# Attention with two-key pooled queries and a gated MLP on one core: products for the maxima inside the groups of scores, two chunks ahead, and values two chunks behind

## The chip, the cores and the metric

One Trainium2 chip, one of its cores. The metric is the time of one execution on the device in microseconds (us), as a median over runs; beside it stands one execution taken with the hardware profiler.

## What is computed

```python
def _attn_ref(q, k, v):                 # q, k, v: 8 x 8 x 1152 x 64, f32
    B, H, S, D = q.shape
    q_pool = q.reshape(B, H, S // 2, 2, D).mean(axis=3)      # 576 queries
    scores = np.matmul(q_pool, k.transpose(0, 1, 3, 2)) / np.sqrt(D)
    scores = scores - np.max(scores, axis=-1, keepdims=True)
    attn = np.exp(scores)
    attn = attn / (np.sum(attn, axis=-1, keepdims=True) + 1e-09)
    return np.matmul(attn, v)

def _moe_ref(x, w_in, w_spatial, b_spatial, w_out):   # x: 8 x 576 x 512
    h = np.maximum(x @ w_in, 0.0)                      # 512 -> 1024
    u, v = h[..., :512], h[..., 512:]
    v_n = (v - mean(v)) / sqrt(var(v) + 1e-06)
    v_s = np.einsum('ts,bsd->btd', w_spatial, v_n) + b_spatial[None, :, None]
    return (u * v_s) @ w_out
```

x is the attention's output with its heads side by side. Results are held to f32 accuracy, so most products are made of three f16 products of high and low halves.

## The kernel before, in words

**Blocks and chunks.** The attention runs over 32 blocks (8 batches times 4 pairs of heads, `NP`). Within a block the 1152 keys are 9 chunks of 128 (`NC`). One chunk is: `scores(i, c)` (line 894), 12 products on TensorE that use 64 rows of the array for each of the two heads, into the tile `pss` (3 PSUM banks, one buffer); one Exp on ScalarE over 1152 columns into `pt` (line 905, 4 buffers); `split(i, c)` (line 913), which takes the low half of `pt`, on GpSimd for eight chunks and on VectorE for one; `values(i, c)` (line 811), 27 products of 128 rows into the tile `o` (2 banks, one buffer). Values lag the scores by one chunk (`LAG`, line 750, used in `attention`). In the first 8 blocks (`EARLY`) three of the nine chunks skip the split, and their values are f32 products.

**The maxima of the next block.** The Exp needs a shift per query, made from the largest score. `maxima(i)` (line 695) computes the scores once more in one f16 product, in 9 pieces of 512 columns for both heads: a pair of 64-row products (two pairs where a piece crosses a tile of queries; line 705) writes both banks of the tile `pm`, and VectorE reduces both heads in one instruction of up to 2 x 512 elements (line 710). Two tail products follow (128 rows, line 717), with their reductions (718). `shift(i)` (line 721) takes the maximum of the pieces (726), writes factors into `wide` (729, 737), turns them with six small products (743, 745), and copies them to `sh` (746, 747). The first chunk's scores of the block read `sh`. The tile `pm` (two banks, one buffer, made by `pair_of_banks`) also serves small jobs: sums for scales, the variance of the MLP, a transposition.

**Where they are put.** The loop at the end makes the generator `ahead_of(i + 1)`: nine pieces, tails, shift. Each of block i's nine chunks steps it once after its scores, and `drain(nxt)` at the end of the block runs what is left: tails and shift. So block i + 1 begins behind them in the program.

**The other work.** `prep(i + 2)` and `steps_of_k(i + 1)` make the f16 halves of queries and keys (line 666 takes a difference of keys on VectorE, 456 and 459 are squares and halves on ScalarE), `values_ahead` those of v (621, 622 and, on GpSimd, 624), all stepped at fixed rates per chunk; the weights are loaded and turned from f64 in the first blocks (474 to 486). Every 8 blocks a `gated_unit`, the MLP of two batches, becomes ready: it makes products into `pw` (one bank, lines 968, 1032, 1083, 1092, 1130), stepped about 20 times per block. The last unit has nothing beside it and runs at the end in all free banks.

**What sets the order.** `Order.pin` takes the whole program and lays it out by list scheduling: it has a cost per instruction, due times, and per engine a list of the ready ones; the earliest start wins, then the lowest number in the program. The order found is then fixed on each engine's queue, which runs in order. Tiles of one name must begin in the order of the program, and a tile waits for all users of the one that had its buffer. A `bundle` is a row of TensorE products placed without a break: the 12 of a chunk's scores, or those of one piece of the maxima. Going from 128-row products to a bundle costs the planner 100 ns for scores and 1500 ns for maxima (`APART`), so it waits that long for something of the same kind.

Of the kernel before, what the change touches and what calls it, by code (L numbers as in the profile page):

```python
# [31 lines left out]
class Order:  # L32
# [8 lines left out]
    APART = {"scores": 100, "maxima": 1500}  # L41
    SIZE = {F16: 2, BF16: 2, F32: 4, I32: 4, U32: 4, I64: 8}

    def __init__(self):
        self.slot = {}
        self.count = {}
        self.lined = []
        self.seen = 0
        self.bundles = []
        self.plan = []  # L50
# [20 lines left out]
    @contextmanager  # L71
    def bundle(self, tc, part):
# [3 lines left out]
        self.bundles.append((part, names))  # L76
# [130 lines left out]
    def pin(self, tc):  # L207
# [18 lines left out]
        members, wait = {}, [0.0] * len(prog)  # L226
        for part, ns in self.bundles:
            ns = [place[x] for x in ns]
            members[ns[0]] = [(n, bool(prog[n].ins) and self.access(prog[n].ins[0])[3] >= 64) for n in ns]
            wait[ns[0]] = self.APART[part]  # L230
            for n in ns:
                lead[n] = ns[0]
# [19 lines left out]
        def placed(n, t, end):  # L252
            e = lane[n]
            if e in last:
                tc.add_manual_dep(prog[n], last[e], dep, reason="order")
            last[e] = prog[n].name
            self.plan.append((prog[n].name, t, end))
            for m, through in after[n]:
                k = lead[m]
                left[k] -= 1  # L260
                if not through:
                    x = t
                elif lane[m] != e:
                    x = end + self.DELAY.get((e, lane[m]), 52)
                else:
                    x = t if e == "PE" else end + 34
                there[k] = max(there[k], x)
                due[k] = max(due[k], x + (self.SLACK.get((e, lane[m]), 0) if through else 0))
                if not left[k]:
                    ready[lane[k]].append(k)  # L270

        while any(ready.values()):
            best = None
            for e, ns in ready.items():
                if ns:

                    at = {n: max(due[n], wire - 1000) if n in load else due[n] for n in ns}
                    if e == "DVE":
                        for n in ns:
                            if shared[n] and max(free[e], at[n]) + self.GRAB >= held[0]:  # L280
                                at[n] = max(at[n], held[1] - 175)
                    elif e == "PE":
                        for n in ns:
                            if (n in members) != halves:
# [10 lines left out]
            if e == "PE":  # L295
                if (n in members) != halves:
                    t = max(free[e] + self.SWITCH, t)
                    halves = not halves
                row, at = [t, t], t
# [27 lines left out]
def attn_sgu_kernel(ctx: ExitStack, tc: tile.TileContext, qT, kT, v, w_in, w_spT, b_sp, w_out, out):  # L327
    nc = tc.nc
    P = 128
# [31 lines left out]
    ps_m = order.pool(ctx.enter_context(tc.tile_pool(name="ps_m", bufs=1, space=PSUM)), 1, True)  # L361
# [62 lines left out]
    def pair_of_banks():  # L424
        return ps_m.tile([P, 2, 512], F32, name="pm")

    def short():
        return pair_of_banks()[:, 0] if units else ps_w.tile([P, 512], F32, name="pw")
# [265 lines left out]

    def maxima(i, banks=None):
# [3 lines left out]
        for n, cols in enumerate(PIECES):  # L699
            pm = banks(n) if banks else pair_of_banks()  # L700
            with order.bundle(tc, "maxima"):
                for t, _, y, z, a in cols:
                    for h in range(2):
                        q = t * P if h == 0 or t < 3 else ROLL + TAIL
                        nc.tensor.matmul(  # L705
                            pm[:, h, a : a + z - y], lhsT=qhi[HEADS[h], q : q + P], rhs=khi[HEADS[h], y:z],
                            start=True, stop=True,
                        )
            for t, k, y, z, a in cols:
                nc.vector.reduce_max(out=mt[:, t : t + 5 : 4, k], in_=pm[:, :, a : a + z - y], axis=AX.X)  # L710
            yield
        for n in range(2):
            pm = banks(n) if banks else pair_of_banks()
            w = 512 if n == 0 else P
            for k in range(2 - n):
                y = (2 * n + k) * 512
                nc.tensor.matmul(pm[:, k, :w], lhsT=qdd, rhs=khi[:, y : y + w], start=True, stop=True)  # L717
            nc.vector.reduce_max(out=mt[:, 8, 2 * n : 2 + n], in_=pm[:, 0 : 2 - n, :w], axis=AX.X)  # L718
        yield

    def shift(i):
        st = state[i]
        mt, w, out = st["mt"], wide[i % 2], sh[i % 2]
        pm = pair_of_banks()
        m = pm[:, 1, 384 : 384 + NT]
# [15 lines left out]
        yield  # L741
        for t in range(3):
            nc.tensor.matmul(pm[:, 0, t * P : (t + 1) * P], lhsT=w[:, t], rhs=ident_h, start=True, stop=True)
        for t, e in ((3, eye[:, HALF : 2 * P]), (4, eye[:, 0 : P + HALF]), (5, rest_eye)):
            nc.tensor.matmul(pm[:, 1, 0 : S - CUT], lhsT=w[:, t], rhs=e, start=t == 3, stop=t == 5)
        nc.vector.tensor_copy(out=out[:, CUT:S], in_=pm[:, 1, 0 : S - CUT])
        nc.vector.tensor_copy(out=out[:, 0:CUT], in_=pm[:, 0, 0:CUT])
        yield

    LAG = 1  # L750
# [122 lines left out]
    def scores(i, c):  # L873
# [17 lines left out]
        with order.bundle(tc, "scores"):  # L891
            for _, h, n, dst, w, m, bank in sorted(todo, key=lambda x: x[:3]):
# [22 lines left out]
    def attention(i):  # L915
        for c in range(NC):
            scores(i, c)
# [8 lines left out]
    def gated_unit(un):  # L926
# [58 lines left out]
        pt = pair_of_banks()[:, 0]  # L985
# [208 lines left out]
    def at_start(n):  # L1194
        return pair_of_banks() if n % 2 == 0 else ps_o.tile([P, 2, 512], F32, name="o")
# [8 lines left out]
    first = maxima(0, at_start)  # L1204
# [6 lines left out]
    drain(first)  # L1211
    drain(shift(0))
# [6 lines left out]
    def ahead_of(i):  # L1219
        yield from maxima(i)  # L1220
        yield
        yield from shift(i)

# [5 lines left out]
    nxt = ahead_of(1)  # L1229
    for i in range(NP):  # L1230
# [7 lines left out]
        for at in attention(i):  # L1238
            if at == "scores":
                nxt = step(nxt)  # L1240
# [6 lines left out]
        drain(nxt)  # L1247
        for r in run[:2]:
            drain(r.gen)
        nxt = ahead_of(i + 2) if i + 2 < NP else None  # L1250
# [55 lines left out]
```

## Time and profile before

| what | us |
|---|---|
| median of 2 runs (1427.98 to 1436.63) | 1432.31 |
| the profiled execution's own time | 1430.54 |
| its span, first to last instruction | 1428.8 |
| TensorE, products busy | 1192.4 (83%) |
| VectorE busy | 909.2 (64%) |
| ScalarE busy | 859.1 (60%) |
| GpSimd busy | 718.7 (50%) |
| first Exp starts at | 35.0 |
| last Exp starts at | 1307.8 |

PE is TensorE, PEld its weight loads, DVE VectorE, ACT ScalarE, POOL GpSimd. A busy TensorE in the page counts a product until its result has landed, so products that overlap look long; what a row of products costs is read from the chain of waits, where each stands with the time it added. A releaser is the instruction whose end let a waiting one go.

### The profile page before, as it was taken

The page shows a single profiled execution, that of the slowest core. Times are in us where ns is not written, and L with a number is a line of the kernel's source. Part 1 is how long each engine was busy: PE and PEld are TensorE (multiplying, and loading weights), DVE is VectorE, ACT ScalarE, POOL GpSimd, SP SyncE. Part 2 cuts the span into 40 slices and gives each one's busy share as a digit, 9 for nine tenths or more (in the row PEclk, how much of TensorE's full clock was granted, in tenths as well). Part 3 has the DMA queues.
Part 4 walks back from the last instruction along what each step waited for, and adds up shares of the span by engine and source line. Part 5 has one row for each costly group of instructions (what it writes and reads, how often), then busy time and mean ns, then how long its engine had stood idle before and what let it go on. Part 6 is the DMA issues. An engine that isn't in the chain of part 4 may idle for free.

```text
span 1428.8 us, 33823 instructions
## 1 busy us (share of the span) xinstructions
PE 1192.4 (83%) x14680; PEld 792.6 (55%) x14680; DVE 909.2 (64%) x1640; ACT 859.1 (60%) x1235; POOL 718.7 (50%) x386
## 2 busy tenths in 40 slices
PE   2787777778989897798998886788998888789988
PEld 1575666666546655555555554555655455556443
DVE  7778667865777666865658665575556856561543
ACT  6755566676756666658666665567666465544333
POOL 1444334454646656656666555756766365645000
PEclk9878889989999998799999997899999898899999
DMA  4530421231211222134221122124111020001001
GB/s 158 209 110 34 144 68 68 68 100 44 75 59 40 87 74 77 33 95 131 75 59 45 49 75 75 59 79 151 53 61 59 25 75 9 10 24 53 8 1 67
DMA packets 64118, 99.64 MB, mean 70 GB/s; under 512 B 34016, under 2 KB 34016, under 8 KB 63456
## 3 DMA queue, kind: packets, MB, share of 16 engines
q1 hardware_dynamic: 63968, 97.47, 21.2%
q8 instruction: 115, 1.88, 0.5%
q14 instruction: 35, 0.29, 0.1%
HBM read 81.20 MB, written 9.44 MB: 63 GB/s over the span
## 4 chain that ended last, share of the span: by engine, by line
PE 57%; DVE 20%; ACT 15%; issue 4%; DMA 2%; POOL 2%; ACTq 0%; DVEq 0%; POOLq 0%
PE pss L894 16%; PE o L811 13%; ACT pt L905 8%; DVE mt L710 4%; PE pw L968 4%; PE pw L1130 4%; PE pw L1083 4%; PE pw L1032 4%; PE pm L705 3%; DVE mt L718 2%; DVE kd L666 2%; POOL pt L913 1%; DVE vv L462 1%; PE pm L717 1%; PE pss L968 1%
## 5 line engine op out<-in xcount | busy, mean ns | idle before, releaser
L913 POOL TENSOR_TENSOR pt<-pt 128x1152 f16<-128x1152 f32 x240 | 518.7, 2163 | 550.3 <-ACT pt L905 549.9
L710 DVE TENSOR_REDUCE mt<-pm 128x2 f32<-128x1024 f32 (+1 forms) x380 | 354.2, 952 | 319.5 <-PE pm L705 318.7
L905 ACT ACTIVATE pt<-pss,esc 128x1152 f32<-128x1152 f32 x288 | 350.6, 1218 | 276.9 <-PE pss L894 267.5
L811 PE MATMUL o<-vp,pt 128*128 128x65 f16 (+3 forms) x7128 | 315.9, 199 | 12.9 <-ACT pt L905 10.3
L811 PEld LDWEIGHTS <-pt 128*128 128x128 bf16 (+1 forms) x7128 | 267.3, 99 | 100.0 <-issue 56.7
L894 PE MATMUL pss<-qh,dh 64*128 64x192 f16 (+1 forms) x1152 | 245.8, 307 | 42.4 <-ACT pt L905 40.5
L894 PE MATMUL pss<-qh,dl 64*128 64x192 f16 (+1 forms) x1152 | 244.5, 304 | 0.0
L894 PEld LDWEIGHTS <-dh 64*128 64x128 f16 x2304 | 180.2, 100 | 112.0 <-issue 86.5
L894 PE MATMUL pss<-ql,dh 64*128 64x192 f16 (+1 forms) x1152 | 240.5, 303 | 0.0
L705 PE MATMUL pm<-kh,qh 64*128 64x512 f16 (+1 forms) x760 | 120.7, 348 | 14.2 <-DVE mt L710 10.7
L894 PEld LDWEIGHTS <-dl 64*128 64x128 f16 x1152 | 92.2, 100 | 3.1 <-issue 0.8
L1032 PE MATMUL pw<-xg,wi_h 128*128 128x512 f16 (+1 forms) x304 | 75.8, 332 | 10.9 <-ACT u L1042 10.9
L1130 PE MATMUL pw<-wo_h,vv 128*128 128x512 f16 x216 | 73.3, 391 | 11.9 <-DVE vv L462 6.5
L705 PEld LDWEIGHTS <-qh 64*128 64x128 f16 x768 | 54.7, 99 | 43.9 <-issue 27.3
L968 PE MATMUL pw<-wi_h,xg 128*128 128x512 f16 x224 | 75.2, 379 | 3.2 <-ACT vv L976 2.4
L624 POOL TENSOR_TENSOR vp<-vt,vp 128x576 f16<-128x576 f32 x48 | 68.3, 1432 | 8.4 <-ACT vp L622 8.2
L1083 PE MATMUL pw<-ws_h,vv 128*128 128x512 f16 x192 | 65.5, 393 | 6.1 <-ACT u L1042 3.2
L1083 PEld LDWEIGHTS <-vv 128*128 128x128 f16 x384 | 35.6, 100 | 52.0 <-issue 21.1
L968 PEld LDWEIGHTS <-xg 128*128 128x128 f16 x432 | 38.3, 97 | 43.4 <-issue 8.1
L811 PE MATMUL o<-row,pt 128*128 128x65 f32 (+1 forms) x432 | 58.8, 290 | 3.7 <-ACT pt L905 3.6
L718 DVE TENSOR_REDUCE mt<-pm 128x2 f32<-128x1024 f32 (+1 forms) x63 | 47.8, 759 | 18.9 <-PE pm L717 18.5
L811 PEld LDWEIGHTS o<-row,pt 128*128 128x128 f32 x432 | 54.4, 203 | 7.2 <-ACT pt L905 4.7
(227 smaller groups left out, 1970.1 us busy)
## 6 DMA issues: line engine op xcount, KB each, us to landing
vt<-in_v_dram SPq DMA_DIRECT2D x56, 576.0 KB, 4.2
qt<-in_qT_dram SPq DMA_DIRECT2D x32, 576.0 KB, 4.7
kt<-in_kT_dram SPq DMA_DIRECT2D x32, 576.0 KB, 4.0
out_dram<-row SPq DMA_DIRECT2D x24, 256.0 KB, 2.2
vv<-in_w_in_dram SPq DMA_DIRECT2D x4, 1024.0 KB, 6.5
xg<-in_v_dram SPq DMA_DIRECT2D x4, 576.0 KB, 6.4
vv<-in_w_out_dram SPq DMA_DIRECT2D x2, 1024.0 KB, 6.1
out_dram<-vv SPq DMA_DIRECT2D x8, 256.0 KB, 2.0
```

Of the source, the lines that this page charges most:

```text
L624: nc.gpsimd.tensor_sub(vp[:, h, :, 0:D], vt[:, h], hd)
L705: nc.tensor.matmul(pm[:, h, a : a + z - y], lhsT=qhi[HEADS[h], q : q + P], rhs=khi[HEADS[h], y:z], start=True, stop=True,)
L710: nc.vector.reduce_max(out=mt[:, t : t + 5 : 4, k], in_=pm[:, :, a : a + z - y], axis=AX.X)
L718: nc.vector.reduce_max(out=mt[:, 8, 2 * n : 2 + n], in_=pm[:, 0 : 2 - n, :w], axis=AX.X)
L811: nc.tensor.matmul(dst, lhsT=weights[:, cols], rhs=rhs, start=first and n in (0, 3), stop=last, skip_group_check=True)
L894: x = nc.tensor.matmul(dst, lhsT=w, rhs=m, start=first, stop=n == len(terms) - 1, skip_group_check=True)
L905: nc.scalar.activation(pt.rearrange("p (b q) -> p b q", b=3), ps[:, :, 0:CUT], AF.Exp, bias=0.0, scale=st["esc"])
L913: eng.tensor_sub(pt.bitcast(F16)[:, 0::2], pt, pt.bitcast(BF16)[:, 1::2])
L968: nc.tensor.matmul(ph, lhsT=xa[:, cc, c0 : c0 + P], rhs=wa[:, cc, DH:DF], start=n == 0, stop=n == 3 * NCC - 1,)
L1032: nc.tensor.matmul(pu[:, : z - a], lhsT=wa[:, cc, fc * P : (fc + 1) * P], rhs=xa[:, cc, a:z], start=n == 0, stop=n == 3 * NCC - 1,)
L1083: nc.tensor.matmul(pv, lhsT=l, rhs=r[:, 0:MAIN], start=n == 0, stop=n == len(ts) - 1)
L1130: nc.tensor.matmul(py, lhsT=ga[:, fc, c0 : c0 + P], rhs=wa[:, fc, :], start=m == 0, stop=m == end - 1)
```

## The change

- **Pieces in the groups.** `scores(i, c, piece)` steps the generator of pieces inside its bundle, so that a piece's products are the last members of the group of scores, and steps it again behind the Exp, which emits the piece's reductions. There is always one piece to a chunk.
- **Two chunks ahead.** Two pieces of block 1 are made alone before the loop. After that chunk c of block i carries piece c + 2 of block i + 1, and its chunks 7 and 8 carry pieces 0 and 1 of block i + 2. `prep(i + 2)` is drained at chunk 7.
- **Two tiles of one bank.** The pool of `pm` has two buffers of one bank each instead of one of two banks. Each head of a piece has a tile of its own and is reduced by itself, so a piece takes two reductions (four where it crosses a tile of queries) in place of one (two). The tails are three products with a reduction each.
- **Tails and shift inside the block.** A tail goes behind the scores of chunks 0, 2 and 4, the first half of the shift behind chunk 6, its second half (products and copies) behind chunk 7. Nothing of them is left to the end of a block.
- **Values lag two chunks**; `pt` keeps its 4 buffers.
- **The planner.** Both kinds of switch cost 100 ns; a bundle may start before a late member is due, by the member's place in it; an Exp that comes due within 500 ns goes ahead of another ScalarE instruction that would run into it. `PACE`, `APART`, `URGENT` and `TIGHT` have values with which they change nothing.

```diff
-    APART = {"scores": 100, "maxima": 1500}
+    TIGHT = 0
+    AHEAD = 500
...
+                x -= lag[m]
                 there[k] = max(there[k], x)
...
+                    if e == "Activation":
+                        for m in ns:
+                            if m in prime and t < at[m] <= t + self.AHEAD and t + cost[n][0] > at[m]:
+                                n, t = m, at[m]
...
-    ps_m = order.pool(ctx.enter_context(tc.tile_pool(name="ps_m", bufs=1, space=PSUM)), 1, True)
+    ps_m = order.pool(ctx.enter_context(tc.tile_pool(name="ps_m", bufs=2, space=PSUM)), 2, True)
...
+    def one_bank():
+        return ps_m.tile([P, 512], F32, name="pm")
...
+    def maxima_alone(i, banks, n):
+        gen = maxima(i, banks)
+        for _ in range(n):
+            with order.bundle(tc, order.SWITCH):
+                next(gen)
+            next(gen)
+            yield gen
+
     def maxima(i, banks=None):
...
-            pm = banks(n) if banks else pair_of_banks()
-            with order.bundle(tc, "maxima"):
-                for t, _, y, z, a in cols:
-                    for h in range(2):
-                        q = t * P if h == 0 or t < 3 else ROLL + TAIL
-                        nc.tensor.matmul(
-                            pm[:, h, a : a + z - y], lhsT=qhi[HEADS[h], q : q + P], rhs=khi[HEADS[h], y:z],
-                            start=True, stop=True,
-                        )
-            for t, k, y, z, a in cols:
-                nc.vector.reduce_max(out=mt[:, t : t + 5 : 4, k], in_=pm[:, :, a : a + z - y], axis=AX.X)
-            yield
...
+            pms = banks(n) if banks else (one_bank(), one_bank())
+            for t, _, y, z, a in cols:
+                for h in range(2):
+                    q = t * P if h == 0 or t < 3 else ROLL + TAIL
+                    nc.tensor.matmul(
+                        pms[h][:, a : a + z - y], lhsT=qhi[HEADS[h], q : q + P], rhs=khi[HEADS[h], y:z],
+                        start=True, stop=True,
+                    )
+            yield
+            for h in range(2):
+                for t, k, y, z, a in cols:
+                    nc.vector.reduce_max(
+                        out=mt[:, t + 4 * h, k : k + 1], in_=pms[h][:, a : a + z - y], axis=AX.X
+                    )
+            yield
+
+    def tail_maxima(i):
+        st = state[i]
+        khi, qdd, mt = kh[i % 2].rearrange("p c k -> p (c k)"), qd[i % 2], st["mt"]
+        for n in range(3):
+            pm = one_bank()
+            w = min(512, KEYS - n * 512)
+            nc.tensor.matmul(pm[:, :w], lhsT=qdd, rhs=khi[:, n * 512 : n * 512 + w], start=True, stop=True)
+            nc.vector.reduce_max(out=mt[:, 8, n : n + 1], in_=pm[:, :w], axis=AX.X)
+            yield
...
-    LAG = 1
+    LAG = 2
+    LEAD = 2
+    TWO_AHEAD = 2 * (NC - LEAD)
+    TAILS_AT = (0, 2, 4, 6)
...
-    def scores(i, c):
+    def scores(i, c, piece):
...
+            next(piece, None)
         pt = pp.tile([P, 2 * S], F32, name="pt")
-        nc.scalar.activation(pt.rearrange("p (b q) -> p b q", b=3), ps[:, :, 0:CUT], AF.Exp, bias=0.0, scale=st["esc"])
+        x = nc.scalar.activation(pt.rearrange("p (b q) -> p b q", b=3), ps[:, :, 0:CUT], AF.Exp, bias=0.0, scale=st["esc"])
+        order.first.append(x.ins.name)
         st["pt"].append(pt)
+        next(piece, None)
...
-    nxt = ahead_of(1)
+    lead = maxima_alone(1, None, LEAD)
+    for _ in range(LEAD):
+        begun = next(lead)
+    ahead = chain(begun, *(maxima(i) for i in range(2, NP)))
     for i in range(NP):
...
-        for at in attention(i):
+        tails = chain(tail_maxima(i + 1), shift(i + 1)) if i + 1 < NP else None
+        for n, at in enumerate(attention(i)):
+            if n == TWO_AHEAD and run[1].gen is not None:
+                drain(run[1].gen)
+                run[1].gen = None
             if at == "scores":
-                nxt = step(nxt)
+                if n // 2 == NC - LEAD:
+                    drain(tails)
+                    tails = None
+                if n // 2 in TAILS_AT:
+                    tails = step(tails)
...
-        drain(nxt)
+        drain(tails)
```

## Rows read from the trace of the kernel before

**Rows 1.** The page, its first part: the span, and busy time and share of each engine.
```profile
span 1428.8 us, 33823 instructions
PE 1192.4 (83%) x14680; PEld 792.6 (55%) x14680; DVE 909.2 (64%) x1640; ACT 859.1 (60%) x1235; POOL 718.7 (50%) x386
```

**Rows 2.** Busy time of each engine in six stretches: block 0, blocks 1 to 7, 8 to 15, 16 to 23, 24 to 31, and what follows the last Exp. Columns: stretch and length in us, then busy us (instructions) of each engine, the granted share of TensorE's clock, DMA share, GB/s.
```profile
35.00:59.50 24.50, 21.09 (x297) 17.58 (x295) 16.39 (x20) 19.54 (x31) 13.36 (x7) 1.00 0.81 301
59.50:330.00 270.50, 206.21 (x2584) 165.95 (x2583) 194.51 (x313) 173.18 (x237) 111.13 (x54) 0.85 0.25 83
330.00:654.30 324.30, 280.78 (x3690) 184.16 (x3690) 221.20 (x396) 209.03 (x300) 195.82 (x103) 0.94 0.22 68
654.30:985.00 330.70, 282.46 (x3727) 184.03 (x3724) 205.87 (x385) 207.64 (x299) 197.50 (x104) 0.94 0.24 71
985.00:1309.00 324.00, 282.65 (x3685) 183.43 (x3683) 191.37 (x359) 188.54 (x257) 190.93 (x99) 0.93 0.16 47
1309.00:1428.80 119.80, 109.01 (x659) 52.81 (x657) 52.35 (x116) 39.02 (x75) 3.27 (x2) 0.99 0.09 30
```

**Rows 3.** The Exps alone (line 905), in stretches laid from one block's last Exp to the next block's first, and, in the second row, over a block's nine. Columns: stretch, length, ScalarE busy (instructions; one cut by the edge counts), clock, DMA.
```profile
222.10:232.10 10.00, 0.04 (x1) 0.83 0.01 2
232.10:255.10 23.00, 10.88 (x9) 1.00 0.39 131
1024.30:1040.00 15.70, 0.00 (x0) 1.00 0.31 93
1235.40:1246.30 10.90, 0.03 (x1) 0.79 0.12 24
```

**Rows 4.** All engines in the same kind of stretches: between blocks 4 and 5 and within block 5 (no MLP unit yet), between 24 and 25 and within 25 (a unit runs), between 29 and 30 and within 30 (the unit waits). Columns as in rows 2.
```profile
222.10:232.10 10.00, 5.55 (x62) 4.10 (x60) 8.81 (x19) 4.86 (x11) 1.18 (x1) 0.83 0.01 2
232.10:255.10 23.00, 19.20 (x300) 16.38 (x298) 18.50 (x26) 16.40 (x20) 12.55 (x6) 1.00 0.39 131
1024.30:1040.00 15.70, 14.15 (x112) 6.96 (x109) 11.29 (x27) 7.21 (x12) 10.45 (x6) 1.00 0.31 93
1040.00:1064.50 24.50, 23.49 (x365) 15.90 (x364) 12.90 (x20) 18.48 (x25) 15.37 (x8) 1.00 0.15 51
1235.40:1246.30 10.90, 5.95 (x65) 4.24 (x66) 6.18 (x18) 2.97 (x5) 7.93 (x5) 0.79 0.12 24
1246.30:1269.20 22.90, 20.22 (x331) 15.44 (x328) 13.80 (x17) 16.13 (x18) 15.08 (x7) 0.88 0.01 3
```

**Rows 5.** The chain of waits across the boundary of blocks 29 and 30. Columns: start us, us, engine, tile and line.
```profile
1236.51 0.34 PE pm L705 x2
1236.87 1.24 DVE mt L710
1238.15 0.61 PE pm L717 x2
1238.78 1.22 DVE mt L718
...
1240.35 0.69 DVE xm L825
1241.04 0.20 DVE mt L718
...
1242.76 0.49 PE pm L745 x3
1243.28 0.36 DVE sh L746
1243.63 0.47 DVE sh L747
```

**Rows 6.** The chain of waits around the boundary of blocks 24 and 25, in the stretches where TensorE's own products are the chain: what each row of products adds.
```profile
1020.62 0.22 PE pm L705 x2
...
1023.13 1.00 PE o L811 x27
1024.13 1.73 PE pw L968 x8
...
1026.98 0.32 PE pm L705 x2
...
1044.97 0.84 PE pss L894 x9
```

**Rows 7.** Groups of instructions by line and shape: the reductions of pieces and tails. Columns: line, engine, operation, out<-in, shapes, count | busy us, mean ns | idle before and its releaser.
```profile
L710 DVE TENSOR_REDUCE mt<-pm 128x2 f32<-128x1024 f32 x188 | 230.1, 1224 | 213.1 <-PE pm L705 212.4
L710 DVE TENSOR_REDUCE mt<-pm 128x2 f32<-128x512 f32 x64 | 41.3, 686 | 28.8 <-PE pm L705 28.8
L718 DVE TENSOR_REDUCE mt<-pm 128x1 f32<-128x128 f32 x31 | 8.8, 283 | 3.1 <-PE pm L717 3.0
```

**Rows 8.** Who waited for whom, in total: engine and line, releaser, us, times, longest.
```profile
POOL pt L913 <- ACT pt L905: 549.9, 207, 18.5
ACT pt L905 <- PE pss L894: 267.5, 197, 6.4
PE pss L894 <- ACT pt L905: 40.5, 57, 2.3
```

**Rows 9.** Groups by line and shape of two other instructions: the split on GpSimd, and the key differences on VectorE.
```profile
L913 POOL TENSOR_TENSOR pt<-pt 128x1152 f16<-128x1152 f32 x240 | 518.7, 2163 | 550.3 <-ACT pt L905 549.9
L666 DVE TENSOR_TENSOR kd<-kt 128x1152 f32<-128x1152 f32 x32 | 51.2, 1600 | 2.0 <-POOL qt L638 1.6
```

More of the change, by code (lines that the diff above doesn't have):

```diff
@@ L49, in __init__ @@
         self.bundles = []
+        self.first = []
         self.plan = []
@@ L71, in bundle @@
     @contextmanager
-    def bundle(self, tc, part):
+    def bundle(self, tc, wait, pace=0):
         first = len(tc.nc.cur_bb.bb.instructions)
@@ L75, in bundle @@
         names = [i.name for i in tc.nc.cur_bb.bb.instructions[first:] if i.engine == tc.nc.tensor.engine]
-        self.bundles.append((part, names))
+        self.bundles.append((wait, pace, names))
     def access(self, x):
@@ L225, in pin @@
         lead = list(range(len(prog)))
-        members, wait = {}, [0.0] * len(prog)
-        for part, ns in self.bundles:
+        members, wait, lag = {}, [0.0] * len(prog), [0.0] * len(prog)
+        paced, turn, tight = {}, 0.0, set()
+        prime = {place[x] for x in self.first}
+        for apart, pace, ns in self.bundles:
             ns = [place[x] for x in ns]
-            members[ns[0]] = [(n, bool(prog[n].ins) and self.access(prog[n].ins[0])[3] >= 64) for n in ns]
-            wait[ns[0]] = self.APART[part]
+            if pace:
+                paced[ns[0]] = pace
+            if apart > self.SWITCH:
+                tight.add(ns[0])
+            members[ns[0]] = [(n, self.access(prog[n].ins[0])[3] >= 64) for n in ns]
+            wait[ns[0]] = apart
+            row, at = [0.0, 0.0], 0.0
+            for n, g in members[ns[0]]:
+                at = lag[n] = max(at, row[g])
+                row[g] = at + self.cost("PE", prog[n])[0]
             for n in ns:
@@ L256, in placed @@
             last[e] = prog[n].name
-            self.plan.append((prog[n].name, t, end))
+            self.plan.append((prog[n].name, t, end, cost[n][0]))
             for m, through in after[n]:
@@ L266, in placed @@
                     x = t if e == "PE" else end + 34
+                x -= lag[m]
                 there[k] = max(there[k], x)
-                due[k] = max(due[k], x + (self.SLACK.get((e, lane[m]), 0) if through else 0))
+                slack = self.TIGHT if k in tight else self.SLACK.get((e, lane[m]), 0)
+                due[k] = max(due[k], x + (slack if through else 0))
                 if not left[k]:
@@ L298, in pin @@
                     halves = not halves
+                if n in paced:
+                    turn = t
                 row, at = [t, t], t
@@ L422, in attn_sgu_kernel @@
     units = []
-    def pair_of_banks():
-        return ps_m.tile([P, 2, 512], F32, name="pm")
+    def one_bank():
+        return ps_m.tile([P, 512], F32, name="pm")
     def short():
-        return pair_of_banks()[:, 0] if units else ps_w.tile([P, 512], F32, name="pw")
+        return one_bank() if units else ps_w.tile([P, 512], F32, name="pw")
     def scales(sq, name, up=0):
@@ L741, in shift @@
         yield
+        pm0 = one_bank()
         for t in range(3):
-            nc.tensor.matmul(pm[:, 0, t * P : (t + 1) * P], lhsT=w[:, t], rhs=ident_h, start=True, stop=True)
+            nc.tensor.matmul(pm0[:, t * P : (t + 1) * P], lhsT=w[:, t], rhs=ident_h, start=True, stop=True)
         for t, e in ((3, eye[:, HALF : 2 * P]), (4, eye[:, 0 : P + HALF]), (5, rest_eye)):
-            nc.tensor.matmul(pm[:, 1, 0 : S - CUT], lhsT=w[:, t], rhs=e, start=t == 3, stop=t == 5)
-        nc.vector.tensor_copy(out=out[:, CUT:S], in_=pm[:, 1, 0 : S - CUT])
-        nc.vector.tensor_copy(out=out[:, 0:CUT], in_=pm[:, 0, 0:CUT])
+            nc.tensor.matmul(pm[:, 0 : S - CUT], lhsT=w[:, t], rhs=e, start=t == 3, stop=t == 5)
+        nc.vector.tensor_copy(out=out[:, CUT:S], in_=pm[:, 0 : S - CUT])
+        nc.vector.tensor_copy(out=out[:, 0:CUT], in_=pm0[:, 0:CUT])
         yield
-    LAG = 1
+    LAG = 2
+    PACE = 0
+    APART = 1500
+    URGENT = 6
+    LEAD = 2
+    TWO_AHEAD = 2 * (NC - LEAD)
+    TAILS_AT = (0, 2, 4, 6)
     SPLIT_DVE = (4,)
@@ L890, in scores @@
                     at += z - y
-        with order.bundle(tc, "scores"):
+        with order.bundle(tc, order.SWITCH, PACE if i >= EARLY else 0):
             for _, h, n, dst, w, m, bank in sorted(todo, key=lambda x: x[:3]):
@@ L916, in attention @@
         for c in range(NC):
-            scores(i, c)
+            scores(i, c, ahead)
             yield "scores"
@@ L1194, in at_start @@
     def at_start(n):
-        return pair_of_banks() if n % 2 == 0 else ps_o.tile([P, 2, 512], F32, name="o")
+        if n % 2 == 0:
+            return one_bank(), one_bank()
+        o = ps_o.tile([P, 2, 512], F32, name="o")
+        return o[:, 0], o[:, 1]
     load_kq(0)
@@ L1203, in attn_sgu_kernel @@
     load_kq(1)
-    first = maxima(0, at_start)
+    first = maxima_alone(0, at_start, 9)
     for _ in range(5):
@@ L1217, in attn_sgu_kernel @@
     credit = 0.0
[L1219 to L1222, printed above, removed]
     def chain(*gens):
```

17 lines of the change are left out of this document (6 added, 11 removed).

## The prediction

> **What bounds the kernel now.** I read the page's first part, then stretches block by block, then the chain across three boundaries, then groups by shape. No engine is full over the whole span: TensorE is busy 83% by a count that lets products overlap, VectorE 64%, ScalarE 60%, GpSimd 50% [rows 1]. The stretches show why. From a block's last Exp to the next block's first there are 10 to 16 us without an Exp; the nine Exps of a block take about 23 to 24.5 us [rows 3]. So some 40 us per block are 24 of flow and 11 to 16 of boundary. Three kinds of boundary must be kept apart [rows 4]. Between blocks 4 and 5, where no MLP unit exists, TensorE is busy 5.55 of 10.0 us and VectorE 8.81: VectorE is the wall. Between 29 and 30, where the unit waits, TensorE is busy 5.95 of 10.9 and VectorE 6.18: nobody is full, it is a chain. Between 24 and 25 a unit runs, and TensorE is busy 14.15 of 15.7: the boundary is filled with MLP products that have to be done anyway, and removing it only moves them. The chain of the empty kind reads [rows 5]: last piece 0.34, its reduction 1.24, tail 0.61, reduction 1.22, the block's normalisation (L825) 0.69, the second tail's reduction 0.20, factors, turning products 0.49, two copies 0.36 and 0.47, and only then the scores. Exps wait 267.5 us in all for scores, and splits 549.9 for Exps [rows 8]: both stand behind it. It is late as a whole because pieces come one per chunk and the tails after the last.
>
> TensorE's true need over blocks 8 to 31, a stretch of 324.3 + 330.7 + 324.0 = 979 us [rows 2], from what rows of products add to the chain [rows 6]: a chunk costs 0.84 (scores) + 0.22 (piece) + 1.00 (values) = 2.06, times 216 chunks 445. An MLP product of 512 columns is 1.73/8 = 0.216; a unit has by the code 108 + 96 + 112 + 108 = 424 of them, 91.7, and 160 short ones at the values' 1.00/27 = 0.037, 5.9: three units 293. Tails and turning products 0.61 + 0.49 [rows 5] per block, 26. Sum 764 at full clock, 764/0.94 = 813 at the clock granted: 83% of 979. The rest, 166 us, is what better order could give back at most there.
>
> **The change part by part.** *Boundary.* With pieces two chunks ahead, block i + 1 has its ninth piece at chunk 6, tails are spread over chunks 0 to 4, and the shift stands at chunks 6 and 7. Before chunk 0 of the next block there is at least one whole chunk of time for copies of 0.36 and 0.47 [rows 5]. The chain no longer holds the scores. What is late next is an engine's own load.
>
> *Middle blocks.* How much idle time stays on TensorE? Within blocks it is idle 1.0 of 24.5 us beside a unit and 2.7 of 22.9 without one [rows 4], 4% and 12%. Time moved out of the boundary must be filled by the same machinery, and VectorE, at 618 us there [rows 2], gets 46 more (below), 75% of what I forecast; I take 10% idle. The clock was 1.00 in three of the six stretches, and 0.79 to 0.88 in the two empty boundaries and in block 30 [rows 4]; with fewer gaps I take 0.96 for 0.94. Then 764/0.96 = 796, divided by 0.90: 884, a gain of 95. Bounds: 4% idle gives 829 (gain 150); 16% idle, today's 17% nearly, gives 947 (32).
>
> *The clock by rule.* In the empty boundaries the granted clock is 0.79 and 0.83 and in the dense stretches beside them 1.00 or 0.88 [rows 4]. The Trainium skill, page "TensorE: Matmul & The Clock Gate", section "Why this matters for your kernels", asks for no idle gaps between bursts so that the array stays at its full clock. By that rule alone, full clock throughout, the middle would be 764/0.90 = 849 and the whole 35 us under my forecast; block 30 at 0.88 without such a gap is why I stop at 0.96.
>
> *Early blocks.* Blocks 1 to 7 take 270.5 us, VectorE 194.5 of them [rows 2]; 13.4 are added, 208. In its dense stretches VectorE is busy 18.50 of 23.0, 80%, in its boundary 88% [rows 4]; spread evenly I take 85%: 245, a gain of 25. Bounds: 92% gives 226 (44), 80% gives 260 (10).
>
> *More reductions.* A reduction of 1024 elements takes 1224 ns and one of 512 takes 686 [rows 7]: 1.05 ns an element and 148 ns fixed (the 128-element one, 283, agrees). Pieces go from 12 to 24 reductions per block, tails from 2 to 3: 13 x 0.148 = 1.92 us per block, 62 in all. VectorE has room for it in the middle (618 + 46 of 884); in early blocks it is counted above. If nothing hid it, it would cost 62. The Trainium skill, page "Perfetto Trace Analysis", section "Optimizing Scalar/DVE Operations", puts the fixed cost of a VectorE access to PSUM near 125 ns and says that larger operations help where the engine is full: it speaks against this part, with an estimate of 52 us by its figure; the same section says that breaking instructions up may let work finish sooner where the engine only makes others wait. The 62 from the rows stand.
>
> *Pieces inside the group.* A piece that stands alone between 128-row products adds 0.32 to 0.34 to the chain, behind scores 0.22 [rows 5, 6]: 0.1 saved per piece that stood alone; between none and all 288 that is 0 to 29 us; it is part of the idle share above, so I add nothing. The cost is a wait: the piece's products stand on TensorE's in-order queue behind scores and ahead of the values and MLP products, and need two free tiles. Each tile is free when its reductions of the piece before are done, 2 x 0.69 after it; the pitch of a chunk will be about 884/216 = 4.1 us, so some 2 us are spare. I take 0; the bound is the rival below.
>
> *Shift across chunk 7.* The shift's tile is held from chunk 6 until its second copy, while chunk 7's piece wants that bank: reductions 1.37, maximum and factors about 1.1, products 0.49, copy 0.36 make 3.3 us against a pitch of 4.1. I take 0; if VectorE is 1.5 us late each time, 31 x 1.5 = 47.
>
> *Values two behind.* A split takes 2.16 on GpSimd [rows 9] after the Exp; at the dense stretches' 23/9 = 2.6 a chunk, a lag of one leaves it little. With two, the split has a chunk more, and `pt`'s four buffers still suffice. I count no gain (bound: half a us in each of 288 chunks that TensorE now waits, 144, were all of the idle time this), and as cost one more row of values after the last Exp, 1.0. *Exp first:* ScalarE may idle up to 0.5 us for it; it is 60% busy [rows 1], and TensorE waits 40.5 us for Exps today [rows 8]. 0, bounds 20 either way.
>
> *Head.* Block 0's maxima take 13 more reductions, 1.9, and two pieces of block 1 stand before the first group, about 0.6 of TensorE: +4 with the last values.
>
> Sum on the profiled execution (1430.5, with a span of 1428.8): 1430.5 - 95 - 25 + 4 = 1314.5; the median of the runs is 1.8 above it, so about 1316.
>
> **The rivals.** *Packed tighter:* 4% idle in the middle (-150) and VectorE 92% in early blocks (-44): 1432 - 194 + 4 = 1242. For it: a dense stretch with a unit does run at 96% [rows 4]. Against: `pss` and `pw` have one buffer each, so a chunk's scores wait for its Exp.
>
> *Only empty boundaries pay:* filled ones return nothing, since the MLP products go elsewhere and meet the same waits. Then 25 early, and about 7 in each of six later blocks without MLP work (from 34 to GpSimd's 584/24 = 24.3 us a block at 90%): 1432 - 25 - 42 + 4 = 1369. For it: 14.15 of 15.7 busy at such a boundary. Against: those units race ahead and then leave blocks without work, so moving their products evens the load.
>
> *VectorE late for the tiles (slower):* each group's last members wait for a VectorE that is in something else, such as the 1.60 of L666 [rows 9]; before, pieces could fall behind without holding scores. Price: 288 groups by the wait. One reduction of 0.69 per group is 199 us: 1515. It cancels the gain from 0.41 a group on. For it: VectorE at 80 to 88% in early blocks. Against: 52 to 60% in the middle's dense stretches, where 216 of the 288 groups are. By the skill's sentence on grouping it would be this one.
>
> *The shift's chain moves* from chunk 0 to chunk 7: the boundary stays under another number, and only what is overlapped goes; with its 47 on top of the case before, 1416: no change.
>
> **How the numbers follow.** Forecast 0.42 (1280 to 1345); packed 0.18; empty boundaries only 0.20; shift moved 0.08; VectorE late 0.12, a quarter of it near cancelling. A measurement of this kernel tells about 2% from no change. Faster: 0.42 + 0.18 + 0.20 = 0.80; same: 0.08 + 0.03 = 0.11; slower 0.09. The time is the likeliest case's, 1316; the range of 1245 to 1405 leaves out about 0.18.
>
> **What would show it.** Right: nine Exps at an even pitch with no gap over 5 us at a block's start; no wait of the turning products for factors that holds scores; TensorE's clock at 0.95 or more in the middle; VectorE's busy time up by about 62 and its share at 70% or more; MLP products in every middle block, not in six of eight. Wrong: long waits of the pieces' products for VectorE (L705's successors), a gap of the same length at chunk 7, or TensorE idle over 15% in the middle. Faster than 1280 would mean that the idle share, slower than 1345 that the coupling to VectorE, was misjudged.

## The result: 1262.87 us, and the profile after

The kernel after takes 1262.87 us (1261.34 to 1264.4, two runs) against 1432.31: a ratio of 0.8817, 95% interval 0.8694 to 0.8940. The forecast was 1316 with a range of 1245 to 1405; the gain is 169 us where 116 were forecast. The profiled execution took 1261.34, with a span of 1258.9.

The page's first part after, to be read beside [rows 1]:

```profile
span 1258.9 us, 34256 instructions
PE 1129.0 (90%) x14680; PEld 762.5 (61%) x14680; DVE 951.9 (76%) x2056; ACT 853.3 (68%) x1235; POOL 730.2 (58%) x386
```

TensorE has the same 14680 products; VectorE has 416 instructions more and is busy 43 us longer. The stretches after, cut like those of [rows 2] (block 0, blocks 1 to 7, blocks 8 to 31 in one, what follows the last Exp); columns are stretch, length, busy us (instructions) of PE, PEld, DVE, ACT, POOL, clock, DMA share, GB/s:

```profile
35.80:71.10 35.30, 27.49 (x318) 21.56 (x317) 28.08 (x50) 25.57 (x41) 14.83 (x7) 0.95 0.58 212
71.10:309.50 238.40, 199.05 (x2574) 162.46 (x2574) 191.75 (x399) 162.84 (x216) 109.16 (x52) 0.89 0.25 84
309.50:1132.00 822.50, 773.56 (x11030) 517.55 (x11029) 650.12 (x1425) 602.35 (x862) 594.86 (x304) 1.00 0.25 75
1132.00:1258.90 126.90, 114.94 (x710) 55.92 (x706) 52.12 (x116) 40.31 (x76) 3.27 (x2) 0.98 0.10 32
```

Block 0 goes from 24.5 to 35.3 us, blocks 1 to 7 from 270.5 to 238.4, blocks 8 to 31 from 979.0 to 822.5, the end from 119.8 to 126.9, and the first Exp starts 0.8 later: +10.8 - 32.1 - 156.5 + 7.1 + 0.8 = -169.9, the difference of the spans. The middle carries it. Of its 156.5 us, 84 are time in which TensorE has no product (979.0 - 845.9 = 133.1 before [rows 2], 822.5 - 773.6 = 48.9 after). The other 72 are shorter busy time for nearly the same products, at a granted clock of 1.00 where it was 0.93 to 0.94.

The chain of waits from the last scores of block 24 to the first of block 25 (start us, us, engine, tile, line), beside [rows 6]:

```profile
893.76 0.84 PE pss L936 x11
894.60 0.22 PE pm L734 x2
894.81 0.75 PE pw L1013 x3
895.57 0.60 PE o L853 x18
896.16 0.22 PE pw L1013
896.38 0.18 PE o L853 x6
896.56 1.09 PE pss L936 x12
897.65 0.22 PE pm L734 x4
```

Scores, a piece, a few MLP products, values, and the next block's scores 2.8 us behind the last: TensorE itself is the chain. Each piece adds 0.22, none 0.32.

### The profile page after: what moved, and what is told of

Read it like the earlier page. It is cut to its first block, busy times and chain, and to the rows that moved or that the text cites. A ratio compares the mean times of both kernels' runs of the same rounds, so it can differ in the third digit from the quotient of the medians.

```text
span 1258.9 us, 34256 instructions
## 1 busy us (share of the span) xinstructions
PE 1129.0 (90%) x14680; PEld 762.5 (61%) x14680; DVE 951.9 (76%) x2056; ACT 853.3 (68%) x1235; POOL 730.2 (58%) x386
## 4 chain that ended last, share of the span: by engine, by line
PE 62%; DVE 27%; ACT 6%; issue 2%; POOL 1%; ACTq 0%; DVEq 0%; POOLq 0%
PE o L853 17%; PE pss L936 15%; DVE mt L741 8%; PE pw L1013 5%; PE pw L1175 5%; PE pw L1128 5%; PE pw L1077 4%; PE pm L734 4%; ACT pt L948 3%; DVE kd L688 2%; DVE vv L484 2%; DVE vv L1055 1%; DVE mt L753 1%; DVE xm L867 1%; PE pss L1013 1%
## 5 line engine op out<-in xcount | busy, mean ns | idle before, releaser
L741 DVE TENSOR_REDUCE mt<-pm 128x1 f32<-128x512 f32 (+1 forms) x760 | 380.0, 547 | 150.1 <-PE pm L734 148.8
L853 PEld LDWEIGHTS <-pt 128*128 128x128 bf16 (+1 forms) x7128 | 276.6, 99 | 118.2 <-issue 48.4
L936 PE MATMUL pss<-qh,dh 64*128 64x192 f16 (+1 forms) x1152 | 226.6, 294 | 6.3 <-ACT pt L948 5.7
L936 PE MATMUL pss<-qh,dl 64*128 64x192 f16 (+1 forms) x1152 | 224.7, 290 | 0.0
L936 PE MATMUL pss<-ql,dh 64*128 64x192 f16 (+1 forms) x1152 | 224.5, 290 | 0.0
L936 PEld LDWEIGHTS <-dh 64*128 64x128 f16 x2304 | 162.9, 95 | 77.4 <-issue 54.3
L660 POOL TENSOR_TENSOR qt<-qt 128x576 f32<-128x576 f32 x32 | 50.3, 1573 | 46.9 <-DMA qt<-in_qT_dram 45.3
L734 PEld LDWEIGHTS <-qh 64*128 64x128 f16 x768 | 60.9, 97 | 22.0 <-issue 12.8
L853 PE MATMUL o<-row,pt 128*128 128x65 f32 (+1 forms) x432 | 68.1, 309 | 3.4 <-ACT pt L948 3.2
L853 PEld LDWEIGHTS o<-row,pt 128*128 128x128 f32 x432 | 61.7, 220 | 13.6 <-issue 7.8
```

What stands on the lines that cost most here:

```text
L660: nc.gpsimd.tensor_add(q0, q0, q1)
L734: nc.tensor.matmul(pms[h][:, a : a + z - y], lhsT=qhi[HEADS[h], q : q + P], rhs=khi[HEADS[h], y:z], start=True, stop=True,)
L741: nc.vector.reduce_max(out=mt[:, t + 4 * h, k : k + 1], in_=pms[h][:, a : a + z - y], axis=AX.X)
L853: nc.tensor.matmul(dst, lhsT=weights[:, cols], rhs=rhs, start=first and n in (0, 3), stop=last, skip_group_check=True)
L936: x = nc.tensor.matmul(dst, lhsT=w, rhs=m, start=first, stop=n == len(terms) - 1, skip_group_check=True)
```

## The experiments

Theory A, with which I went into them, is the prediction's: the gain is that the shift no longer stands between two blocks. All ratios are to the kernel before, run on the same chip beside each run (medians 1425.5 to 1427.3 us); 95% intervals in brackets. Times of stretches and chunks are read from one trace of each kernel.

**1. No lead** (1233.15; 0.8632 [0.8589, 0.8676]).

```diff
-    LEAD = 2
+    LEAD = 0
...
-    TAILS_AT = (0, 2, 4, 6)
+    TAILS_AT = (2, 4, 6, 8)
...
-    for _ in range(LEAD):
-        begun = next(lead)
+    begun = maxima(1)
```

> The kernel after (1263 us) with no lead: chunk c carries piece c of the next block, tails go behind chunks 2, 4 and 6, the shift's first half behind chunk 8 and its second at the block's end; all else stays. Theory A (the gain is that the shift no longer stands between two blocks): the chain of piece 8, two reductions 1.37, maximum and factors 1.1, turning products 0.5 and copies 0.8 is back before each block's first scores, so some 4 to 5 us in 31 boundaries: 1263 + 140 = 1400, range 1360 to 1430, with empty boundaries and a clock of 0.92 to 0.95 in the middle. Theory B (the gain is the even pace, one piece in each group of scores, and the lag): the lead adds little, 1270 to 1310.

It is faster than the kernel after, so theory A, which is also the prediction's, falls. A small boundary is there again (block 23's last Exp ends at 835.46 and the next starts at 839.67; after has 862.76 and 864.70), and the middle is 6 us longer; the early part is faster, 218.3 for blocks 1 to 7. The stretches of this run, blocks 0, 1 to 7, and 8 to 31:

```profile
33.60:60.50 26.90, 22.98 (x313) 18.48 (x310) 21.25 (x40) 22.42 (x36) 14.92 (x8) 1.00 0.81 305
60.50:278.80 218.30, 185.03 (x2564) 151.55 (x2564) 185.45 (x399) 160.58 (x216) 104.18 (x51) 0.95 0.25 81
278.80:1107.50 828.70, 780.02 (x11049) 522.66 (x11048) 647.79 (x1439) 606.73 (x867) 591.52 (x305) 0.99 0.26 77
```

**2. Pieces as groups of their own, at 100 ns** (1243.22; 0.8710 [0.8678, 0.8743]).

```diff
-            next(piece, None)
+        with order.bundle(tc, order.SWITCH):
+            next(piece, None)
```

> The kernel after with each piece's products as a group of their own behind the scores (switch 100), lead, lag and tiles kept. Theory A: the membership only saves about 0.1 us where a piece stood alone: 1263 to 1290. Theory B (membership makes the pace): pieces fall behind again, 1320 or more. If members hold TensorE's queue for VectorE (the rival of the prediction), freeing them would make it faster, 1230 to 1255, above all in blocks 1 to 7.

Membership isn't the gain either. Block 0, blocks 1 to 7 and blocks 8 to 31 of this run:

```profile
34.00:57.50 23.50, 21.80 (x300) 17.65 (x296) 19.13 (x35) 17.75 (x25) 14.46 (x7) 1.00 0.71 270
57.50:271.80 214.30, 189.59 (x2586) 150.04 (x2585) 194.55 (x413) 165.69 (x224) 113.84 (x53) 0.96 0.28 93
271.80:1112.20 840.40, 802.59 (x11038) 518.79 (x11038) 650.86 (x1429) 607.05 (x870) 585.58 (x305) 0.99 0.26 76
```

Blocks 1 to 7 take 214.3 us by their Exps against 238.4, and block 0 takes 23.5 against 35.3: there the kernel with membership takes 36 us longer. In the middle it takes 18 less (822.5 against 840.4). For the early cost I take the prediction's slower rival, scores that wait for a piece whose tiles VectorE has not freed, in the early blocks alone and not with 199 us; that it is this wait is argued, not shown.

**3. One tile, one joint reduction** (1263.25; 0.8848 [0.8816, 0.8881]).

```diff
-            pms = banks(n) if banks else (one_bank(), one_bank())
+            pm = banks(n) if banks else pair_of_banks()
...
-            for h in range(2):
-                for t, k, y, z, a in cols:
...
+            for t, k, y, z, a in cols:
+                nc.vector.reduce_max(out=mt[:, t : t + 5 : 4, k], in_=pm[:, :, a : a + z - y], axis=AX.X)
...
```

> The kernel after with one tile of two banks and one reduction over both heads, as before (tails two, as before), lead, membership and lag kept. It takes 62 us of VectorE's 952 away, but a piece's tile is free only after the one long reduction, and small jobs share the one buffer. Theory A (VectorE's extra work is hidden, the two tiles give slack): 1275 to 1310. Rival (the 62 us cost time in the early blocks and at chunk 3): faster than now, 1230 to 1255.

Neither: no difference from after that can be told in the whole. VectorE is busy 917.8 us in it against 951.9. Its stretches, as in run 2:

```profile
36.20:63.10 26.90, 24.05 (x318) 18.69 (x317) 19.70 (x32) 22.79 (x36) 12.17 (x7) 1.00 0.71 257
63.10:292.80 229.70, 192.34 (x2578) 154.82 (x2576) 189.12 (x312) 164.59 (x220) 105.88 (x53) 0.93 0.26 87
292.80:1132.00 839.20, 780.00 (x11025) 521.42 (x11026) 627.02 (x1128) 602.52 (x864) 594.07 (x304) 0.99 0.25 74
```

In these traces the equal times hide a trade: the joint form is 17 us faster in blocks 0 to 7, where the rival looked, and 17 us slower in the middle. Tiles and reductions were changed together, so which of them does what is open.

**4. Values one chunk behind** (1267.38; 0.8872 [0.8835, 0.8909]).

```diff
-    LAG = 2
+    LAG = 1
```

> The kernel after with values one chunk behind in place of two. Theory A: values then wait for GpSimd's split (2.19 us after an Exp of 1.22) where the pitch is under 3.4; the mean pitch is 3.8, so little: 1265 to 1295. Theory C (the lag carries much of the gain, since TensorE had nothing ready in a chunk): 1320 or more.

4 us by the medians, within the intervals, as theory A said. So four parts were each undone alone, and the gain stayed each time. Among what these kernels still shared, beside spread tails and Exps going first, was that no piece is held back by the planner's 1500 ns. In the trace of before that hold can be seen. VectorE's and TensorE's timelines between blocks 24 and 25 (start us, us, engine, line, operation, count); the block's last Exp ends at 1024.26:

```profile
1027.34 1.23 DVE L710 TENSOR_REDUCE mt<-pm 128x2 f32<-128x1024 f32 x1 [2.64 <-PE pm L705]
```

```profile
1028.83 0.38 PE L968 MATMUL pw<-wi_h,xg 128*128 128x512 f16 x1 [0.48 <-ACT vv L976]
1029.04 0.38 PE L968 MATMUL pw<-wi_l,xg 128*128 128x512 f16 x1
...
1030.65 0.39 PE L705 MATMUL pm<-kh,qh 64*128 64x512 f16 x2
```

The eighth piece's reduction ends at 1028.57 and sets the tile free; the ninth piece comes at 1030.65, 2.1 us later, behind eight MLP products. From the starts of pieces and Exps over blocks 8 to 30, the lateness grows within a block: the first piece starts 0.3 us ahead of its chunk's Exp in the kernel before, and the ninth 6.0 after it. In the kernel after the ninth starts 0.3 ahead. The next runs test that.

**5. Before, with 100 ns in place of 1500** (1317.70; 0.9240 [0.9189, 0.9290]).

```diff
-    APART = {"scores": 100, "maxima": 1500}
+    APART = {"scores": 100, "maxima": 100}
```

> The kernel before (1432, 1426 beside the last runs) with one number of the planner changed: a piece of the maxima pays 100 ns in place of 1500 for a switch of the array's halves, as scores do. No lead, one joint reduction, values one behind, tails and shift at the block's end. New theory D (the runs without lead, without membership, with a joint tile and with lag one all kept the gain, so what they share is it; they share that no piece waits up to 1500 ns to be placed): 1270 to 1330. Rival E (several parts each break the boundary's chain, and none is enough alone): 1390 to 1430.

One number of the planner gives 108 us. The ninth piece now starts 1.1 us after its Exp, and from a block's last Exp to the end of the next one's first it takes 11.9 us where it took 16.8 (means of blocks 8 to 31, from end to end). The middle's stretch, and the chain at a block whose last Exp ends at 946.81:

```profile
321.70:1196.40 874.70, 814.24 (x11090) 526.09 (x11090) 620.41 (x1138) 602.94 (x861) 586.49 (x304) 0.99 0.23 69
```

```profile
945.87 0.32 PE pm L705 x2
946.19 0.70 PE o L811 x18
946.89 0.43 PE pw L968 x2
947.32 0.78 PE o L811 x24
948.11 0.43 PE pm L717 x2
```

The last piece stands before the block's last Exp has ended, though it still adds 0.32. What is left of the boundary, up to the next Exp at 955.40, is tails, shift, and what stands between them in the same queues (MLP products, the normalisation).

**6. After, own groups at 1500 ns** (1391.04; 0.9745 [0.9703, 0.9788]). The edit is shown against run 2; two planner lines that treat groups with a longer wait apart are left out too, so that the wait is all that differs.

```diff
-        with order.bundle(tc, order.SWITCH):
+        with order.bundle(tc, 1500):
             next(piece, None)
```

> The kernel after with each piece's products as a group of their own that pays 1500 ns, as before; lead, two tiles, tails within the block, lag two and Exp first kept. It differs from the run with groups of their own (1243) in that number alone. Theory D: pieces fall behind their chunks again, 9 x 1.4 us a block at most; with two chunks of lead part of it is hidden: 1290 to 1400. If the lead makes it harmless: 1235 to 1260.

Against run 2 this number alone costs 148 us. The lead does not make it harmless: the ninth piece starts 11.2 us after the Exp of the chunk that carries it, so two chunks of lead are used up. From a block's last Exp to the next one's first it takes 15.7 us again, against 6.4 in run 2. The middle:

```profile
310.00:1261.30 951.30, 832.08 (x11050) 537.84 (x11050) 642.66 (x1439) 611.68 (x869) 590.18 (x305) 0.94 0.23 66
```

**7. No Exp first** (1272.58; 0.8925 [0.8880, 0.8969]).

```diff
-    AHEAD = 500
+    AHEAD = 0
```

> The kernel after without the planner's rule that an Exp due within 500 ns goes first. Theory D: the rule is a detail, ScalarE is 68% busy: 1260 to 1280. Rival F (Exps held up behind other ScalarE work made the boundaries, and this rule is the gain): 1330 or more.

About 10 us slower, and the interval overlaps that of after: a detail at most. Rival F falls.

**8. Before, with the lead alone** (1431.75; 1.0037 [1.0017, 1.0058]).

```diff
-    nxt = ahead_of(1)
+    begun = maxima(1)
+    for _ in range(LEAD):
+        next(begun)
+    ahead = chain(begun, *(maxima(i) for i in range(2, NP)))
...
             if at == "scores":
-                nxt = step(nxt)
+                ahead = step(ahead)
+                if n // 2 == NC - LEAD:
+                    drain(tails)
...
+                if n // 2 in (0, 3, 6):
+                    tails = step(tails)
```

> The kernel before with the lead alone: pieces two chunks ahead, the first tail behind chunk 0 and the second behind chunk 3, the shift behind chunks 6 and 7; pieces stay groups of their own with 1500 ns, one tile of two banks, lag one. My first theory A (the shift's place between blocks was the cost): 1300 to 1340. Theory D (the 1500 ns hold every piece, and through the one tile the next ones): 1380 to 1430, with the gap moved to chunk 7.

Nothing, as theory D said, though the gap did not move to chunk 7: the first Exp of a block ends 15.5 us behind the last one's end, as a mean of blocks 8 to 31, where it was 16.8. Its ninth piece is 14.6 us behind its chunk. Blocks 1 to 7 and 8 to 31:

```profile
60.50:348.50 288.00, 218.30 (x2580) 173.70 (x2579) 197.15 (x312) 171.04 (x232) 108.76 (x53) 0.79 0.23 77
348.50:1303.50 955.00, 833.54 (x11074) 541.74 (x11074) 611.44 (x1139) 604.72 (x856) 583.81 (x304) 0.94 0.21 63
```

**9. Before, with membership alone** (1338.25; 0.9363 [0.9304, 0.9422]). No lead, joint tile, lag one, tails at the block's end, no Exp first:

```diff
-    def scores(i, c):
+    def scores(i, c, piece):
...
+            next(piece, None)
...
+        next(piece, None)
```

The first `next` stands inside the group, the second behind the Exp. The planner's rule that a group may start before a late member is due comes with it.

> The kernel before with membership alone: each piece's products are members of its chunk's group of scores, no lead, one tile of two banks with a joint reduction, tails and shift all at the block's end, values one behind, no Exp first. Theory D (what cost was that pieces were late against their chunk): a member cannot be late, so at least what 100 ns gave, 1318, and up to what the run without lead gave, 1233: 1270 to 1320. If membership only works with the two tiles or the lag: 1340 or more, with TensorE waiting for VectorE behind the scores.

Between the two cases, just short of the second's 1340: membership frees the pieces of the 1500 ns as well (the ninth starts 0.3 us ahead of its Exp), but gives 20 us less than the number does.

**10. Run 5 with its tails spread** (1301.56; 0.9101 [0.9047, 0.9156]).

```diff
-                nxt = step(nxt)
+                ahead = step(ahead)
...
+                if n // 2 in (3, 6, 8):
+                    tails = step(tails)
```

> The kernel before with 100 ns (1318) and its tails behind chunks 3 and 6 and the shift's first half behind chunk 8, in place of all of them at the block's end; lag one, joint tile, pieces as own groups. Two tail products and reductions of 0.6 + 1.2 + 0.3 leave the boundary, some 2 us in 31 boundaries of which half is covered: 1270 to 1305. If the pieces set the boundary alone, the tails are covered: 1310 to 1325.

16 us, by the first theory.

**11. Run 10 with values two behind** (1258.72; 0.8800 [0.8744, 0.8856]).

```diff
-    LAG = 1
+    LAG = 2
```

> The run before this one with values two chunks behind. The lag was worth 4 us in the kernel after (1267 with one, 1263 with two), where another chunk's work stood around it. If it is a detail here too: within 10 us of the run with tails spread. If it opens the first chunks of a block, where TensorE otherwise waits for the split: 25 us less or more.

43 us: the second theory's size, but not its place. Blocks 8 to 31 of run 10 and of this run:

```profile
290.00:1174.50 884.50, 812.23 (x11084) 525.06 (x11084) 630.38 (x1137) 603.72 (x866) 587.33 (x304) 0.98 0.24 71
284.20:1131.60 847.40, 800.48 (x11059) 522.79 (x11057) 614.25 (x1131) 598.68 (x860) 589.94 (x304) 0.98 0.25 73
```

As means over these blocks, the boundary goes from 9.7 to 9.2 us and the rest of a block from 27.2 to 26.1, spread over its chunks. With three small edits the kernel before is where the change is, without membership, lead, a second tile or the Exp rule.

**12. After, no lead and own groups** (1239.70; 0.8671 [0.8624, 0.8717]). The edits of runs 1 and 2 together.

> The kernel after without lead and with pieces as groups of their own at 100 ns: two tiles, tails within the block, lag two, Exp first. Each of the two undone alone was faster than the kernel after (1233 without lead, 1243 with own groups). If both stand for the same thing, a scores group held by a piece that waits: 1230 to 1245. If they add up: 1210 to 1225. If without either the pieces fall behind: 1260 to 1290.

They don't add, as the first case had it; that both stand for a held scores group is not shown by that. Its boundary is 8.6 us where that of after is 3.3, and yet its middle takes 826.7 us against 822.5: a boundary that TensorE fills costs little (it has no product for 15 of the 178 us of these boundaries). Run 1, the kernel after without its lead, is the fastest of all at 1233.15, and its interval lies below that of after.

## Why the prediction was right in its number and wrong in its cause

**Right:** that the time lay in the boundaries without Exps (of the 133 us without a product in the middle before, 98 lay between a block's last Exp and the next one's first; after, 0.7 of 49). Filled ones paid too: 58 of the 98 us lay in the 17 boundaries that hold 20 or more MLP products, so "only empty boundaries pay" fell. The shift behind chunks 6 and 7 did not bring the whole boundary back, but part of it moved there: against run 1 and in the middle, the boundary is 3.3 us instead of 6.3, and chunk 7's Exp comes 5.0 us behind chunk 6's instead of 3.1. VectorE's extra work cost no time in the whole (run 3).

**The step that failed** is the one on the boundary: "It is late as a whole because pieces come one per chunk and the tails after the last", and from it "With pieces two chunks ahead ... The chain no longer holds the scores". The lead alone gave nothing (run 8), and in the kernel after it costs about 26 us by the ratios (run 1). The pieces were late because the planner held each up to 1500 ns before it let the array's halves switch (runs 5 and 6). The tails after the last piece did hold the boundary, with 16 us (run 10). The number stood in the part on the planner; the prediction priced only the switch, 0.1 us (0.32 for a piece between 128-row products, 0.22 behind scores [rows 6]), and not the wait that avoids it, 15 times as long. The Trainium skill, page "TensorEngine Tiling (Array Packing)", section "Key Properties", says that a change of tiling mode drains TensorE. The two rows are in line with that and price it.

That the number came within the range is luck as far as the cause goes: the same change took away the wait, for a reason that the prediction did not give. With lead, two tiles, spread tails and lag two, but with the wait kept (and so without membership), the time is 1391.04 (run 6).

**The middle's size.** Forecast 884 at a clock of 0.96 and 10% idle; measured 822.5 at 1.00, so the 764 us of need are 93% of it. With 0.96 and 7% it would be 856: of the 62 us between, the clock is 34. The Trainium skill, page "TensorE: Matmul & The Clock Gate", section "Why this matters for your kernels", by which the prediction worked out 849, was the nearer guide, and the middle's 1.00 agrees with it. [rows 4] showed 0.88 in block 30, and I let that one row decide.

**Early blocks.** 238.4 for a forecast of 245, but block 0's 10.8 us were not priced, and the end took 7.1, not about 1. In block 4 VectorE is the chain in front of the scores of chunk 7, as the slower rival and that of the moved shift had it: pieces' reductions stand behind the weights' 3.06 us (L484), and the shift behind them. The chain there:

```profile
191.62 1.28 DVE mt L741 x2
192.90 3.06 DVE wi_l L484
195.96 1.21 DVE mt L741 x2
...
197.19 0.20 DVE pm L761
```

That the lead's cost, 20 us in blocks 1 to 7 and 8 in block 0 between runs 1 and after, comes from the shift's place or from keys wanted earlier is only argued; no run tells these apart. The traces speak for the shift: in blocks 0 to 7 TensorE waits 10.0 us for the shift's factors in the kernel after (7 times, up to 3.5) and 0.7 in run 1, and in blocks 1 to 7 chunk 7 comes 4.8 us behind chunk 6 against 2.8.

**More reductions.** Counted right (416), sized wrong: 62 forecast, 34 more busy time between run 3 and after, 82 ns each instead of 148, and no time in the whole. The last part says why.

**Lag and Exp first.** Both taken as 0. The Exp rule is about 10, within its bound. The lag is worth 4 beside the other parts (run 4) and 43 in run 11; a part's worth depends on what stands around it, and I priced it in one place only. Why it is so much there stays open.

**The waits** that were to show it, beside [rows 8]:

```profile
POOL pt L958 <- ACT pt L948: 333.4, 144, 10.0
ACT pt L948 <- PE pss L936: 186.7, 169, 5.0
PE pss L936 <- ACT pt L948: 7.0, 11, 1.3
PE pm L734 <- DVE mt L741: 1.9, 5, 0.7
PE pm L752 <- DVE mt L741: 13.5, 16, 2.7
PE pm L781 <- DVE wide L772: 13.5, 10, 3.5
```

Scores wait 7.0 us for Exps where they waited 40.5, and pieces' products 1.9 for reductions: as a wait on the queue, the slower rival's price is near nothing. Tails (L752) wait 13.5 for reductions. The turning products' wait for factors, which was to be gone, is 13.5 us in its largest row (L781). Before it was:

```profile
PE pm L743 <- DVE wide L737: 43.0, 21, 4.2
```

VectorE's share of 76% came as forecast; its busy time rose by 43, not 62.

## What to carry to other kernels

Where an order is planned, a penalty that the planner avoids by waiting is a stall: price the wait it permits, not the switch it saves, and look in the trace for work whose inputs were long ready. When a change has several parts, undo each, but also do each alone: undoing one showed nothing here, since two of them, the number and membership, removed the same hold. A boundary that is filled with other work still pays when an engine's total need is well below the stretch.

## What was not expected of the hardware

Two reductions of 512 elements in a row cost less than two by themselves. The profile gives 682 ns for one and 1224 for one of 1024 [rows 7], so two should be 1364. Behind a wait, the two of a piece take 1.29 us from the start of the first to the end of the second, against 1.24 for a joint one in the chain [rows 5]. A pair on VectorE's timeline after (start us, us, engine, line, operation, count, idle before):

```profile
201.66 1.29 DVE L741 TENSOR_REDUCE mt<-pm 128x1 f32<-128x512 f32 x2 [0.90 <-PE pm L734]
```

The 62 such pairs of that trace take 1289 ns in the mean, so splitting adds some 65 ns and not 140. Reductions after, by shape:

```profile
L741 DVE TENSOR_REDUCE mt<-pm 128x1 f32<-128x512 f32 x376 | 241.9, 682 | 87.7 <-PE pm L734 87.1
L741 DVE TENSOR_REDUCE mt<-pm 128x1 f32<-128x384 f32 x128 | 70.2, 549 | 23.0 <-PE pm L734 22.8
L741 DVE TENSOR_REDUCE mt<-pm 128x1 f32<-128x128 f32 x128 | 36.1, 282 | 36.8 <-PE pm L734 36.8
```

The 376 of the first row are busy 241.9, less than 376 x 0.682 = 256: neighbours overlap. Of the fixed 148 ns, read from single ones, about half is paid again by a second reduction right behind the first.
